# Token blocks of 512 in place of 384 in an attention and two-FFN kernel on one core

## The chip, the cores and the metric

The kernel runs on one core of a Trainium2 chip. The metric is device time in microseconds (us), the median of several executions. Engines are named as the profile does: PE is TensorE's matmuls, PEld its weight loads, DVE is VectorE, ACT is ScalarE, POOL is GpSimd, SP is SyncE, whose queue issues nearly all transfers. L93 is line 93 of the kernel file.

## What is computed

Attention over chunks of 32 queries with 8 memory keys, 16 keys of left and 8 of right context, for 4 batches, 8 heads, 768 tokens, 64 dimensions; then two feed-forward networks on the 3072 tokens, each 512 to 2048 to 512, in float32:

```
x   = attention(q, k, v, mem_k, mem_v)        # 3072 x 512
h   = x @ w_in1                               # up 1
x   = (s * max(h, 0)**2 + b) @ w_out1         # down 1
h   = x @ w_in2                               # up 2
out = (h - tanh(h)) @ w_out2                  # down 2
```

## The kernel before

Every product of the FFNs is made of three matmuls of float32r halves (`three`, L93 to L95): high weight by high token, low weight by high token, high weight by low token. Each loads its own 128 x 128 weights and streams NB = 384 tokens into one PSUM bank. The down products go through a seven-product scheme of the Winograd kind (P1 to P7): `combine` (L323, on POOL) makes the sums of up's outputs, which go through DRAM (o1, o2) to the down stages.

The stages follow each other, and a scheduler places every engine's instructions by readiness, so that work of one stage appears between that of another:

- Attention runs in 24 units of 128 tokens. `scores` (L181) makes 32 small matmuls into banks 0 and 1; VectorE adds the mask (L190), takes the maximum (L195), scales it (L196); ScalarE makes eight exponentials (L199), which read the scores with scale 0.125 and leave sums; VectorE adds 1e-9 to those sums (L204) and inverts them (L205); the product (L207) is on VectorE for the units of the first block and on POOL for the others. `transposes` (L215, L216) and `values` (L228) follow; ScalarE and VectorE split the result into halves xh and xl (L242, L243).
- Up 1 takes blocks of NB tokens, 16 tiles of 12 matmuls each. A tile is one bank of three (5 to 7). ScalarE's ReLU reads the bank and writes r (L317); VectorE squares r and scales it by s (L319). Attention units of the next block run between the tiles. The first block needs its units, three of them, before it can start, and eight weight conversions (`make_pair`, `to_f32`: L102 on ScalarE; L103, L104, L107 on VectorE; L276 on ScalarE; L277 on POOL).
- Eight quadrants of the down weights (L268 loads, the same conversion into zq) use the two raw buffers after the eight up weights.
- Down 1 and down 2 (`Down`) run through 7 products, 4 groups of 768 tokens, 2 halves of the depth, in 112 entries of 12 matmuls. Each entry's tokens are loaded, split by ScalarE (L411, L416) and VectorE (L412, L417) two entries ahead, into a ring of three. Four pairs of banks take the groups in turn. Products are combined by VectorE from the banks (L481 to L490, L591 to L600).
- Up 2 (L622 to L657) runs 8 weights by 4 groups, each two tiles of 24 matmuls, tanh on ScalarE (L637) and a subtraction on VectorE that reads the bank (L638).

All buffers are named places in one arena, E (2048 words), F (1536), Z (1024), G (768) and H (384).

Of the kernel before, what the change touches and what calls it, by code (L numbers as in the profile page):

```python
# [8 lines left out]
F32 = mybir.dt.float32  # L9
# [16 lines left out]
NB = 384  # L26
# [15 lines left out]
def tile_chunk_attention_two_ffn(  # L42
# [30 lines left out]
    SIZE = {"E": 2048, "F": 1536, "Z": 1024, "G": 768, "H": 384}  # L73

    def new(place, n, dt, name):
        assert n <= SIZE[place[0]], (place, n)
        return arena.tile([P, n], dt, tag=place, name=name)
# [19 lines left out]
    def to_f32(z, raw):  # L97
# [16 lines left out]
    A_QK, A_V = ("F8", "F9", "F10"), ("Z8", "Z9", "Z10")  # L114
    A_X = (("F0", "F1"), ("F2", "F3"))
    A_OT = (("F4", "F5"), ("F6", "F7"))
    A_PT, A_Z = ("Z11", "Z12"), ("Z13", "Z14")
    A_SM, A_R = ("G0", "G1"), ("H0", "H1", "H2")
    Z1 = {("A11", 0): "Z0", ("A11", 1): "Z1", ("A21", 0): "Z2", ("A21", 1): "Z3",
          ("A12", 0): "Z4", ("A12", 1): "Z5", ("A22", 0): "Z6", ("A22", 1): "Z7"}  # L120
    B_S = (("Z8", "Z9"), ("Z10", "Z11"))
    B_WHL = (("E8", "E9"), ("E0", "E1"))
    B_STREAM = ("F0", "F1", "E2", "E3")
    B_RING = (("F8", None), ("F9", None), ("F10", None))
    B_ACC = {"X": ("F2", "F3"), "U": ("F4", "F5"), "V": ("F6", "F7")}
# [12 lines left out]
    D_S = (("Z4", "Z5"), ("Z2", "Z6"))
    D_ACC = {"X": ("F6", "F2"), "U": ("F4", "F0"), "V": ("F1", "F8")}
    D_OUT = ("F9", "F10")  # L140
# [32 lines left out]
    def scores(u):  # L173
# [133 lines left out]
    def up1_tile(j, f, dst):  # L307
# [4 lines left out]
        ps = bank(5 + hcount[0] % 3)[:, 0:NB]  # L312
# [5 lines left out]
        r2 = r.rearrange("p (n t) -> p n t", n=2)  # L318
        nc.vector.scalar_tensor_tensor(out=dst, in0=r2, scalar=s_c[:, 0:1], in1=r2, op0=ALU.mult, op1=ALU.mult)  # L319
# [9 lines left out]
    class Down:  # L329
# [70 lines left out]
        def split(self, i):  # L400
            p, g, h, e = self.entries[i]
            src = self.view(self.part[i // 2], e)
            a, b_ = self.ring[i % len(self.ring)]
            if b_ is None:
                both = new(a, 4 * NB, F32R, "ring")
                xh, xl = both[:, 0:2 * NB], both[:, 2 * NB:4 * NB]
            else:
                xh, xl = new(a, 2 * NB, F32R, "ringh"), new(b_, 2 * NB, F32R, "ringl")
            xh, xl = (t.rearrange("p (x t) -> p x t", x=2) for t in (xh, xl))
# [41 lines left out]
    class Sums:  # L451
# [5 lines left out]
        def at(self, k, g):  # L457
            if (k, g // 2) not in self.t:
# [99 lines left out]
    def w2_load(n):  # L558
        w2[n] = load_raw(wi2, n, C_RAW)
# [168 lines left out]
```

## Time and profile before

| | us |
|---|---|
| three runs | 1148.92, 1149.27, 1150.51 |
| median | 1149.27 |
| span of the profiled execution, first to last instruction | 1147.0 |
| PE busy | 1101.0 |
| VectorE busy | 714.9 |
| ScalarE busy | 508.5 |
| POOL busy | 480.6 |

The profile is of one execution, for which only the span is given: the times of the runs also hold what surrounds the instructions. Busy time of PE counts overlapping matmuls once, so a PE that is busy throughout can still run at different speeds; the distance between starts tells that. A line of waits says which engine's instruction waited for which, the total, how often, and the longest.

### The profile page before, as it was taken

Reading aid. Unit: us, or ns where it says so; the run is one execution under the profiler, and the core shown is the slowest. Engines: PE = TensorE matmul, PEld = TensorE weight load, DVE = VectorE, ACT = ScalarE, POOL = GpSimd, SP = SyncE. Lnnn points to the kernel's source line nnn. Section 1 sums busy time; section 2 is a strip of 40 time slices with the busy share of each in tenths; the row PEclk is TensorE's granted clock in tenths of the full one; section 3 lists DMA queues with packets and bytes.
Section 4 is the critical chain, followed back from the end, with each engine's and each line's share of the span. In section 5 each row is a group of like instructions: output and inputs, shape, how many; then the busy total and the mean of one; then the engine's idle time right before and its main releaser. Section 6 shows DMA issues by size and latency. Waiting matters only on the chain.

```text
span 1147.0 us, 18807 instructions
## 1 busy us (share of the span) xinstructions
PE 1101.0 (96%) x7488; PEld 1075.3 (94%) x7488; DVE 714.9 (62%) x755; ACT 508.5 (44%) x973; POOL 480.6 (42%) x361
## 2 busy tenths in 40 slices
PE   3697899999999999999999999999999999999998
PEld 3596899999999999999999999999999999999998
DVE  5899855555555757668787654355522676677654
ACT  4664544444443345445565333222322454444442
POOL 2365754544548833111010256546756941111100
PEclk9998999999999999999999999999999999999999
DMA  8568665655623775555556366757644976667772
GB/s 329 181 222 305 240 218 198 217 190 200 219 111 146 257 259 172 190 189 193 193 187 218 122 225 242 256 201 249 239 189 164 321 235 192 187 214 224 246 232 83
DMA packets 91895, 242.39 MB, mean 211 GB/s; under 512 B 6560, under 2 KB 63904, under 8 KB 87712
## 3 DMA queue, kind: packets, MB, share of 16 engines
q1 hardware_dynamic: 91472, 240.02, 60.6%
q8 instruction: 58, 0.95, 0.3%
q10 hardware_dynamic: 336, 1.18, 0.3%
q14 instruction: 29, 0.24, 0.1%
HBM read 146.80 MB, written 94.37 MB: 210 GB/s over the span
## 4 chain that ended last, share of the span: by engine, by line
PE 85%; DVE 9%; DMA 2%; ACT 2%; issue 1%; SPq 0%; DVEq 0%; ACTq 0%
PE pb L93 27%; PE pb L95 27%; PE pb L94 27%; PE pb L228 2%; PE pb L215 2%; PE pb L181 1%; DMA raw<-in_wo_dram 1%; DVE oa L319 1%; DMA raw<-in_wi_dram 1%; DVE ring L412 1%; DVE z L107 1%; DVE z L104 1%; ACT sm L199 1%; DVE ringl L417 1%; DVE zq L104 1%
## 5 line engine op out<-in xcount | busy, mean ns | idle before, releaser
L93 PE MATMUL pb<-xh,w 128*128 128x384 f32 x512 | 179.1, 350 | 11.9 <-ACT r L317 7.6
L323 POOL TENSOR_TENSOR ob<-oa 128x384 f32<-128x384 f32 x128 | 148.8, 1163 | 94.0 <-DVE oa L319 68.2
L417 DVE TENSOR_TENSOR ringl<-part,ringh 128x768 fp32r<-128x768 f32 x112 | 137.1, 1237 | 68.2 <-ACT ringh L416 67.9
L94 PE MATMUL pb<-xh,w 128*128 128x384 f32 x512 | 173.8, 339 | 0.0
L95 PE MATMUL pb<-xl,w 128*128 128x384 f32 x512 | 173.1, 339 | 0.0
L94 PE MATMUL pb<-x2h,w 128*128 128x384 f32 x512 | 171.0, 334 | 0.0
L93 PE MATMUL pb<-x2h,w 128*128 128x384 f32 x512 | 170.8, 334 | 0.0
L319 DVE SCALAR_TENSOR_TENSOR oa<-r,s_c 128x384 f32<-128x384 f32 x128 | 118.5, 939 | 70.8 <-ACT r L317 59.5
L416 ACT ACTIVATE ringh<-part 128x768 fp32r<-128x768 f32 x112 | 94.9, 848 | 125.5 <-PE pb L94 120.7
L94 PE MATMUL pb<-ringh,whl 128*128 128x384 f32 x448 | 149.7, 334 | 0.0
L93 PE MATMUL pb<-ringh,whl 128*128 128x384 f32 x448 | 149.7, 334 | 0.0
L94 PE MATMUL pb<-ring,whl 128*128 128x384 f32 x448 | 149.7, 334 | 0.0
L93 PE MATMUL pb<-ring,whl 128*128 128x384 f32 x448 | 149.7, 334 | 0.0
L95 PE MATMUL pb<-ring,whl 128*128 128x384 f32 x448 | 132.9, 336 | 1.5 <-DVE ring L412 1.5
L95 PE MATMUL pb<-ringl,whl 128*128 128x384 f32 x448 | 132.7, 335 | 1.0 <-DVE ringl L417 0.9
L638 DVE TENSOR_TENSOR oa<-pb,r 128x768 f32<-128x768 f32 x64 | 60.4, 954 | 100.3 <-ACT r L637 85.5
L317 ACT ACTIVATE r<-pb 128x384 f32<-128x384 f32 x128 | 61.5, 488 | 133.3 <-PE pb L95 127.1
L323 POOL TENSOR_TENSOR ob<-oa,ob 128x384 f32<-128x384 f32 x64 | 72.6, 1135 | 114.1 <-DVE oa L638 73.3
L93 PEld LDWEIGHTS pb<-xh,w 128*128 128x128 f32 x512 | 97.9, 191 | 16.4 <-ACT r L317 8.4
L637 ACT ACTIVATE r<-pb 128x768 f32<-128x768 f32 x64 | 51.7, 812 | 129.0 <-PE pb L95 127.4
L395 POOL TENSOR_TENSOR whl<-s,whl 128x1024 fp32r<-128x1024 f32 x16 | 43.8, 2735 | 147.1 <-ACT whl L394 147.1
L412 DVE SCALAR_TENSOR_TENSOR ring<-part,b_c,ring 128x768 fp32r<-128x768 f32 x64 | 75.5, 1188 | 37.2 <-ACT ring L411 37.0
(93 smaller groups left out, 2239.9 us busy)
## 6 DMA issues: line engine op xcount, KB each, us to landing
o<-ob SPq DMA_DIRECT2D x64, 768.0 KB, 4.1
part<-o SPq DMA_DIRECT2D x112, 384.0 KB, 3.9
part<-o SPq DMA_DIRECT2D x56, 768.0 KB, 4.5
o<-oa SPq DMA_DIRECT2D x64, 576.0 KB, 3.4
raw<-in_wi_dram SPq DMA_DIRECT2D x16, 1024.0 KB, 6.4
raw<-in_wo_dram SPq DMA_DIRECT2D x16, 1024.0 KB, 6.5
qk<-in_qk_dram SPq DMA_DIRECT2D x24, 640.0 KB, 4.5
v<-in_vw_dram SPq DMA_DIRECT2D x21, 384.0 KB, 3.6
```

The lines of the kernel that those rows point to most:

```text
L93: nc.tensor.matmul(acc, lhsT=whi, rhs=xhi, start=first, stop=False)
L94: nc.tensor.matmul(acc, lhsT=wlo, rhs=xhi, start=False, stop=False)
L95: nc.tensor.matmul(acc, lhsT=whi, rhs=xlo, start=False, stop=last)
L317: nc.scalar.activation(out=r, in_=ps, func=AF.Relu)
L319: nc.vector.scalar_tensor_tensor(out=dst, in0=r2, scalar=s_c[:, 0:1], in1=r2, op0=ALU.mult, op1=ALU.mult)
L323: sub = lambda o, x, y: eng.tensor_tensor(out=o, in0=x, in1=y, op=ALU.subtract)
L395: eng.tensor_tensor(out=w[:, 1024:2048], in0=src, in1=w[:, 0:1024].bitcast(F32), op=ALU.subtract)
L412: nc.vector.scalar_tensor_tensor(out=xl, in0=src, scalar=self.bias, in1=xh.bitcast(F32), op0=ALU.add, op1=ALU.subtract)
L416: nc.scalar.activation(out=xh, in_=src, func=AF.Copy)
L417: nc.vector.tensor_tensor(out=xl, in0=src, in1=xh.bitcast(F32), op=ALU.subtract)
L637: nc.scalar.activation(out=r, in_=ps[:, :, 0:NB], func=AF.Tanh)
L638: nc.vector.tensor_tensor(out=oa[:, 2 * i:2 * i + 2], in0=ps[:, :, 0:NB], in1=r, op=ALU.subtract)
```

## The change

A block is 512 tokens, so every FFN matmul streams 512 columns into a whole bank. There are 6 blocks of up 1 in place of 8, 3 groups in place of 4 in both down stages and in up 2, 84 entries per down stage in place of 112, each still of 12 matmuls. The FFN matmuls are 4320 in place of 5760. The first block needs four attention units. Places are laid out anew: E and Z remain in the arena, the others lie in a side pool that holds Q, S, R (attention and ReLU buffers) until up 1 is through and Y (sums) after it. The pairs of float32r halves lie in one buffer or in two, as the place has room (`pair`).

The square in up 1 takes one factor from the bank and one from r, in place of both from r, so the bank is read twice. The mask's adding multiplies the scores by 0.125 as well, the maximum's own scaling is gone, and the exponentials take scale 1. Six of the eight down 1 quadrants are loaded in blocks 1 to 3 of the code and two in the last block; those of down 2 have raw buffers of their own.

```diff
-NB = 384
+NB = 512
...
-    SIZE = {"E": 2048, "F": 1536, "Z": 1024, "G": 768, "H": 384}
+    SIZE = {"E": 2048, "Z": 1024, "Y": 1024, "Q": 1280, "S": 768, "R": 512}
...
+    def swap_side(letters):
+        if "pool" in side:
+            side["pool"].__exit__(None, None, None)
+        side["pool"] = tc.tile_pool(name="side_" + letters[0], bufs=1, reuse_waits="tile")
+        side["of"] = side["pool"].__enter__()
...
-            nc.vector.tensor_tensor(
+            nc.vector.scalar_tensor_tensor(
                 out=sm[:, 4 * g:4 * g + 4, :], in0=bank(g)[:, 0:4 * KE].rearrange("p (r k) -> p r k", r=4),
-                in1=m4, op=ALU.add,
+                scalar=scale, in1=m4, op0=ALU.mult, op1=ALU.add,
             )
...
-        nc.vector.tensor_single_scalar(nmx, nmx, scale, op=ALU.mult)
...
-                bias=nmx[:, h:h + 1], scale=scale, accum_out=sums[:, h:h + 1],
+                bias=nmx[:, h:h + 1], scale=1.0, accum_out=sums[:, h:h + 1],
...
-        ps = bank(5 + hcount[0] % 3)[:, 0:NB]
+        ps = bank(5 + hcount[0] % 3)
...
-        r2 = r.rearrange("p (n t) -> p n t", n=2)
-        nc.vector.scalar_tensor_tensor(out=dst, in0=r2, scalar=s_c[:, 0:1], in1=r2, op0=ALU.mult, op1=ALU.mult)
+        ps2, r2 = (t.rearrange("p (n t) -> p n t", n=2) for t in (ps, r))
+        nc.vector.scalar_tensor_tensor(out=dst, in0=ps2, scalar=s_c[:, 0:1], in1=r2, op0=ALU.mult, op1=ALU.mult)
...
-                if 3 <= j <= 6 and i4 == 1 and q in (0, 2):
-                    thunks.append(down1.load_quadrant(A_RAW[q // 2]))
-                if 3 <= j <= 6 and i4 == 3 and q in (0, 2):
-                    thunks.pop()()
+                if (j in (1, 2, 3) and q in (0, 2)) or (j == NBLK - 1 and q in (0, 1)):
+                    if i4 == 1:
+                        thunks.append(down1.load_quadrant(A_RAW[1 if j == NBLK - 1 else q // 2]))
+                    if i4 == 3:
+                        thunks.pop()()
```

In the order that the scheduler gives, two places matter here. The first is TensorE's order up to the first FFN matmul. Scores have 64x96 operands, transposes 96x128, values 64x64; the numbers after qk, sm and v tell the units apart. Before, it ends so:

```order
L181 MATMUL pb_69<-qk_325 64x96 x16
L215 MATMUL pb_69<-ident_82,sm_278 96x128 x8
L228 MATMUL pb_69<-pt_251,v_117 64x64 x16
L181 MATMUL pb_69<-qk_403 64x96 x16
L228 MATMUL pb_69<-pt_329,v_123 64x64 x16
L93 MATMUL pb_69<-xh_243,w_133 128x384
```

Now it ends so:

```order
L247 MATMUL pb_69<-pt_326,v_123 64x64 x16
L201 MATMUL pb_69<-qk_399 64x96 x16
L234 MATMUL pb_69<-ident_82,sm_353 96x128 x8
L201 MATMUL pb_69<-qk_476 64x96 x8
L247 MATMUL pb_69<-pt_403,v_246 64x64
L234 MATMUL pb_69<-ident_82,sm_430 96x128 x4
L201 MATMUL pb_69<-qk_476 64x96 x3
L247 MATMUL pb_69<-pt_403,v_246 64x64 x15
L234 MATMUL pb_69<-ident_82,sm_430 96x128 x4
L201 MATMUL pb_69<-qk_476 64x96 x5
L234 MATMUL pb_69<-ident_82,sm_541 96x128 x4
L201 MATMUL pb_69<-qk_594 64x96 x8
```

Behind the values of the third unit (v_123) there now stand, ahead of the first FFN matmul, the values of a fourth (v_246), and scores and transposes of later units; in all 7.5 scores, 5.5 transposes and 4 values against 6, 3 and 3 (x16 of scores or values is one unit, x8 of transposes too).

The second is ScalarE's order within block 0: conversions of down weights (zq) among the ReLUs (r), the exponentials (sm) and the copies of attention (pt, xh). Before:

```order
L317 ACTIVATE r_703<-pb_69 128x384
L317 ACTIVATE r_720<-pb_69 128x384
L216 ACTIVATE pt_735<-pb_69 96x512 x2
L102 ACTIVATE zq_2505<-raw_2449 128x1024
L317 ACTIVATE r_754<-pb_69 128x384
L317 ACTIVATE r_804<-pb_69 128x384
L317 ACTIVATE r_835<-pb_69 128x384
L102 ACTIVATE zq_2762<-raw_2695 128x1024
```

Now:

```order
L336 ACTIVATE r_598<-pb_69 128x512
L336 ACTIVATE r_632<-pb_69 128x512
L116 ACTIVATE zq_2061<-raw_1984 128x1024
L336 ACTIVATE r_681<-pb_69 128x512
L261 ACTIVATE xh_590<-pb_69 128x4x128
L116 ACTIVATE zq_2306<-raw_2239 128x1024
L336 ACTIVATE r_718<-pb_69 128x512
L336 ACTIVATE r_733<-pb_69 128x512
```

Two or so ReLUs still stand between two conversions, but each is of a 512-column tile, and six conversions are here, where there were eight.

## Rows read from the trace of the kernel before

**Rows 1.** The page, part 1: TensorE's busy time, share, instructions
```profile
PE 1101.0 (96%) x7488; PEld 1075.3 (94%) x7488; DVE 714.9 (62%) x755; ACT 508.5 (44%) x973; POOL 480.6 (42%) x361
```

**Rows 2.** Busy times by stretch: length, PE, PEld, DVE, ACT, POOL, clock, DMA
```profile
52.10:142.00 89.90, 79.53 (x652) 74.05 (x652) 84.23 (x88) 47.94 (x122) 55.97 (x33) 0.94 0.70 245
142.00:440.00 298.00, 297.87 (x2503) 284.99 (x2504) 168.76 (x231) 139.42 (x419) 163.09 (x132) 1.00 0.55 199
```

**Rows 3.** Timeline of PE in down 1: start, duration in us
```profile
599.96 0.33 PE L93 MATMUL pb<-ring,whl 128*128 128x384 f32 x1
...
605.85 0.33 PE L95 MATMUL pb<-ring,whl 128*128 128x384 f32 x1
```

**Rows 4.** Timeline of PE at half clock, in block 0
```profile
107.36 0.52 PE L94 MATMUL pb<-xh,w 128*128 128x384 f32 x1
...
109.92 0.52 PE L93 MATMUL pb<-xh,w 128*128 128x384 f32 x1
```

**Rows 5.** Timeline of PE and PEld after an attention piece in up 1
```profile
265.60 0.19 PEld L93 LDWEIGHTS pb<-xh,w 128*128 128x128 f32 x1
265.71 0.19 PEld L94 LDWEIGHTS pb<-xh,w 128*128 128x128 f32 x1
265.88 0.34 PE L94 MATMUL pb<-xh,w 128*128 128x384 f32 x1
```

**Rows 6.** Timeline of PE in the opening: values, first FFN matmul
```profile
24.50 1.97 PE L228 MATMUL pb<-pt,v 96*64 96x64 f32 x30 [0.31 <-ACT pt L216]
...
45.85 1.98 PE L228 MATMUL pb<-pt,v 96*64 96x64 f32 x32 [2.49 <-DVE xl L243]
52.11 0.69 PE L93 MATMUL pb<-xh,w 128*128 128x384 f32 x1 [4.29 <-ACT xh L242]
```

**Rows 7.** The maximum's scaling, L196: duration ns min/median/max
```profile
L196 DVE TENSOR_SCALAR nmx<-nmx x24: 157/171/2361, 10.9 to 353.3; 128x8 f32<-128x8 f32 x24
```

**Rows 8.** Timeline of PE around values, and around transposes and scores
```profile
252.74 0.34 PE L95 MATMUL pb<-xl,w 128*128 128x384 f32 x1
...
254.37 0.34 PE L94 MATMUL pb<-xh,w 128*128 128x384 f32 x1
...
259.57 0.34 PE L94 MATMUL pb<-xh,w 128*128 128x384 f32 x1
...
262.52 0.34 PE L94 MATMUL pb<-xh,w 128*128 128x384 f32 x1
```

**Rows 9.** Groups by line, PE, 52.1 to 142 us: count, busy us, mean ns
```profile
L93 PE MATMUL pb<-xh,w 128*128 128x384 f32 x108 | 40.0, 371 | 11.7 <-ACT r L317 7.4 <-ACT xh L242 4.3
...
L215 PE MATMUL pb<-ident,sm 128*96 128x128 f32 x40 | 6.6, 320 | 2.9 <-POOL sm L207 2.9
L228 PE MATMUL pb<-pt,v 96*64 96x64 f32 x160 | 6.3, 226 | 0.0
L181 PE MATMUL pb<-qk 64*64 64x96 f32 x128 | 3.9, 250 | 0.0
```

**Rows 10.** Waits, 52 to 142 us: total us, times, longest
```profile
ACT zq L102 <- DMA raw<-in_wo_dram: 17.7, 7, 6.1
...
PE pb L93 <- ACT r L317: 7.4, 3, 3.8
```

**Rows 11.** Timeline of SP: issues of raw down weights, first and eighth
```profile
68.72 0.33 SPq L268 DMA_DIRECT2D raw<-in_wo_dram  x1
...
121.05 0.33 SPq L268 DMA_DIRECT2D raw<-in_wo_dram  x1
```

**Rows 12.** Timeline at the end: the last VectorE instruction
```profile
1142.68 0.95 DVE L596 TENSOR_TENSOR o<-sumU,pb 128x768 f32<-128x768 f32 x1 [4.58 <-PE pb L95]
```

**Rows 13.** VectorE reading a bank, 512 columns, L243: duration ns min/median/max
```profile
L243 DVE TENSOR_TENSOR xl<-pb,xh x24: 632/680/692, 35.8 to 371.4; 128x512 fp32r<-128x512 f32 x24
```

**Rows 14.** The page, part 5: a down split's VectorE half
```profile
L417 DVE TENSOR_TENSOR ringl<-part,ringh 128x768 fp32r<-128x768 f32 x112 | 137.1, 1237 | 68.2 <-ACT ringh L416 67.9
```

**Rows 15.** Waits, 142 to 440 us
```profile
DVE sums L204 <- ACT sm L199: 37.2, 16, 3.4
```

More of the change, by code (lines that the diff above doesn't have):

```diff
@@ L69, in tile_chunk_attention_two_ffn @@
     pb = psum.tile([P, 8 * 512], F32, name="pb")
-    SIZE = {"E": 2048, "F": 1536, "Z": 1024, "G": 768, "H": 384}
+    SIZE = {"E": 2048, "Z": 1024, "Y": 1024, "Q": 1280, "S": 768, "R": 512}
+    side = {}
+    def swap_side(letters):
[3 more added lines that the diff above has]
+        side["of"] = side["pool"].__enter__()
+        side["letters"] = letters
+    swap_side("QSR")
+    ctx.callback(lambda: side["pool"].__exit__(None, None, None))
     def new(place, n, dt, name):
         assert n <= SIZE[place[0]], (place, n)
-        return arena.tile([P, n], dt, tag=place, name=name)
+        if place[0] in "QSRY":
+            assert place[0] in side["letters"], place
+        pool = arena if place[0] in "EZ" else side["of"]
+        return pool.tile([P, n], dt, tag=place, name=name)
     def bank(k):
@@ new lines, in tile_chunk_attention_two_ffn, with pair @@
+    D_WHL = (("E8", "E10"), ("E2", "E3"))
+    D_STREAM = ("E0", "E1", "E6", "E14", "E17")
+    D_RING = (("Z5", "Z11"), "E13", "E16")
+    D_S = (("Z9", "Z10"), ("Z2", "Z3"))
+    D_ACC = {"X": ("Z7", "Z8", "Z4"), "U": ("Z6", "Z0", "Z1"), "V": ("Y0", "Y1", "E7")}
+    D_OUT = ("E9", "E15")
+    def pair(place, n, names):
+        if isinstance(place, tuple):
+            return tuple(new(p_, n, F32R, nm) for p_, nm in zip(place, names))
+        both = new(place, 2 * n, F32R, "".join(names))
+        return both[:, 0:n], both[:, n:2 * n]
@@ L402, in split @@
             src = self.view(self.part[i // 2], e)
[L403 to L409, printed above, removed]
+            xh, xl = (
+                t.rearrange("p (x t) -> p x t", x=2)
+                for t in pair(self.ring[i % len(self.ring)], 2 * NB, ("ringh", "ringl"))
+            )
             if self.bias is not None and ORDER[p] in ("P1", "P2", "P3", "P6"):
@@ L457, in at @@
         def at(self, k, g):
-            if (k, g // 2) not in self.t:
-                self.t[k, g // 2] = new(self.places[k][g // 2], 4 * NB, self.dt, f"sum{k}")
-            o = 2 * NB * (g % 2)
-            return self.t[k, g // 2][:, o:o + 2 * NB].rearrange("p (m t) -> p m t", m=2)
+            place = self.places[k][g]
+            if (k, place) not in self.t:
+                n = 2 * NB * self.places[k].count(place)
+                self.t[k, place] = new(place, n, self.dt, f"sum{k}")
+            o = 2 * NB * (g - self.places[k].index(place))
+            return self.t[k, place][:, o:o + 2 * NB].rearrange("p (m t) -> p m t", m=2)
     def load1(dst, name, g, h):
@@ L466, in load1 @@
             nc.sync.dma_start(
[L467 removed]
+                out=dst[:, 2 * NB * jj:2 * NB * (jj + 1)].rearrange("p (q t) -> p q t", q=2),
                 in_=o1[2 * g + jj][:, 2 * h:2 * h + 2, SLOT[name], :],
             )
[L471 to L472 removed]
+    sums1 = Sums(B_ACC, F32)
+    x2 = {}
     def final1(name, g, ps):
@@ L477, in last_sum @@
         def last_sum(k, x, op):
-            o = new(B_TMP[n_tmp[0] % 2], 2 * NB, F32, "x2").rearrange("p (m t) -> p m t", m=2)
-            n_tmp[0] += 1
+            o = a(x)
+            if k == "Q":
+                o = new(B_TMP[g], 2 * NB, F32, "q").rearrange("p (m t) -> p m t", m=2)
             nc.vector.tensor_tensor(out=o, in0=a(x), in1=ps, op=op)
-            hi = new(B_HI[k][g], 2 * NB, F32R, "x2h").rearrange("p (m t) -> p m t", m=2)
+            hi, lo = (
+                t.rearrange("p (m t) -> p m t", m=2) for t in pair(X2[k][g], 2 * NB, ("x2h", "x2l"))
+            )
             nc.scalar.activation(out=hi, in_=o, func=AF.Copy)
-            lo = lows1.at(k, g)
             nc.vector.tensor_tensor(out=lo, in0=o, in1=hi.bitcast(F32), op=ALU.subtract)
@@ L645, in tile_chunk_attention_two_ffn @@
                 w2_make(n + 1)
-            if g == 2 and n < 4:
-                thunks.append(down2.load_quadrant(C_RAW))
-            if g == 3 and n < 4:
-                thunks.pop()()
-            if n in (4, 5, 6) and g in (2, 3):
-                if down2.quads:
-                    down2.load_quadrant(C_RAW)()
+            if g == 0 and 1 <= n <= 4:
+                thunks.extend(down2.load_quadrant(C_RAW[1 + i]) for i in range(2))
+            if g in (1, 2) and thunks:
+                thunks.pop(0)()
             if n == 7 and g in (1, 2):
```

55 lines of the change are left out of this document (23 added, 32 removed).

## The prediction

> **What bounds the kernel now.** I began with the busy time per engine: TensorE works for 1101.0 of 1147.0 us [rows 1]. That share hides two regimes, so I then read the busy times by stretch [rows 2]. From 142 us TensorE never pauses (297.87 of 298.00 us), and no other engine sets the time. Between 52.1 and 142 us VectorE is the one without a pause (84.23 of 89.90), TensorE stands for a tenth of the stretch, and its clock falls to 0.94 on average. Before 52.1 us no FFN matmul has run at all.
>
> In the saturated part the question is what one matmul costs, and its duration does not answer that, since matmuls overlap. The timeline does: 34 matmuls of 384 columns start between 599.96 and 605.85 us [rows 3], 173.2 ns apart. At 2.4 GHz 384 columns take 160 ns, so 13.2 ns of each step are not columns. Where the clock is at its lower level, 1.2 GHz, eight steps take 2.56 us [rows 4], 320 ns each, which is 384 columns and nothing else. So the 13.2 ns show at full clock only, and one size cannot say what they depend on. There are three readings: a fixed amount per matmul; an amount that grows with the columns; or a floor of about 173 ns that a longer matmul would clear. For the floor speaks that a weight load (0.19 us) lasts about as long as a step. Against it: after a pause, the load at 265.60 lets the next load begin at 265.71 and the second matmul at 265.88 [rows 5]. With a step of 173 between the two matmuls the first must have begun near 265.71, 0.11 us after its own load began, so weights are ready long before 160 ns are over. I take the fixed amount.
>
> **The matmuls.** Blocks of 512 leave the columns alone and cut the FFN matmuls from 5760 to 4320. Before: 5760 x 0.1732 = 997.6 us. After, with the same 13.2 ns on 213.3 ns of columns: 4320 x 0.2265 = 978.5 us. The gain is 1440 x 13.2 ns = **19.1 us**. The ends are the other two readings: 0.1732 x 512/384 = 0.2309, which gains nothing, and 213.3 ns without any extra, 921.5 us, which gains 76.
>
> The Trainium skill ("TensorE: Matmul & The Clock Gate", section "Wait — 56ns, not 53.3ns?") also has an extra that vanishes at the low clock, and the same one at 128 and 512 columns, but of 2.5 ns. By that rule 4320 steps would take 215.8 ns each, 932 us in all. The trace differs already at 384 columns: the rule would give 162.5 ns, the row 173.2.
>
> **The opening.** Block 0 of up 1 needs four attention units in place of three. Values matmuls of units 0 to 2 start 24.50 to 45.85 us, 10.7 us apart, and the first FFN matmul at 52.11 [rows 6]. A fourth unit at that pace would give 62.8. The scale in the mask's adding removes the tiny scaling of the maximum, which usually takes 0.17 us but up to 2.36 [rows 7] when VectorE is held up; I give it back 2 to 3 us in the opening and take **60 us**, so +7.9. Bounds: 56, if the new order packs better (the weight conversions fill VectorE's pauses), and 68, if the one to two more weight conversions that now stand ahead of the fourth unit on VectorE all count.
>
> Part of this is work that no longer has to be done later. In the order, 7.5 score groups, 5.5 transposes and 4 values stand ahead of the first FFN matmul, against 6, 3 and 3. Prices from the timeline: values push the matmuls apart by 1.63 less two steps = 1.28 us; transposes and scores together by 2.95 less six steps (1.04) = 1.91 us, about 0.9 and 1.0 [rows 8]. So 1.5 x 1.0 + 2.5 x 0.9 + 1.28 = **-5.0 us**.
>
> **Blocks 0 and 1.** Between 52.1 and 142 us 108 x 3 FFN matmuls ran, and 5 transposes, 5 values, 4 score groups [rows 9]: 324 x 0.1732 + 5 x 1.28 + 4 x 1.91 + 0.9 = 71.0 us. So 18.9 of 89.9 us were lost. The waits name the cause: ScalarE waits 17.7 us for raw down weights, and TensorE's first matmuls of a tile wait for the ReLU that frees their bank [rows 10]. ScalarE runs in order, so a ReLU behind a conversion that waits for its transfer waits too. Transfers of the eight quadrants are issued from 68.72 to 121.05 us, 7.5 us apart [rows 11]; there are two raw buffers, so each waits for a conversion. The order lets about two ReLUs through per conversion: two tiles, 24 x 0.1732 = 4.2 us and 1.2 us of attention (3 units x 3.19 over 16 tiles). 5.4 against 7.5 loses 2.1 a time, eight times 17 us, near the 18.9. After: two tiles take 24 x 0.2265 = 5.4 us and 1.6 us of attention (4 units over 16 tiles), 7.0 against 7.5; and only six quadrants come here, two now in the last block. 0.5 x 6 = 3 us, the 2 us that the estimate lacked above, and 3 us because the square now reads the bank, so the bank is free one VectorE instruction later. I take **8 us lost, so -10.9**. Bounds: 4, and 19 as now.
>
> **The rest.** The last VectorE add takes 0.95 us for 768 columns [rows 12]; 1024 add about 0.3, the last store as much: **+0.5 us**. The square at 512 columns from the bank has a near row, a subtraction of 512 columns from the bank at 0.680 us [rows 13]; it is cover work, TensorE needs 2.7 us a tile. In the down stages a split's VectorE half takes 1.24 us for 768 columns [rows 14], about 1.6 for 1024, under twelve matmuls of 2.7 us (2.1 now): the same share, nothing on the path. Without that cover it would cost the difference at each of 168 splits. In the new order up 2's first half that uses the last down 1 group's bank is put behind its sister half, so that hand-over costs nothing. Token loads and stores keep their bytes.
>
> **The sum:** -19.1 + 7.9 - 5.0 - 10.9 + 0.5 = -26.6 us, against the profiled span of 1147.0: 1120.4. The median of the runs, 1149.27, lies 2.3 us above that span, for what surrounds it; the forecast is 1149.27 - 26.6 = **1123 us**. Within this case the opening (-4 to +8) and block 0 (-4 to +11) give 1114 to 1143.
>
> **Rivals.**
>
> *Floor or a smaller extra:* a step of 215.8 ns. 932.3 in place of 978.5: 46 us less, **1077 us**. For it speaks the length of the weight load, and that the extra vanishes at half clock, as a floor would; against it, that weights were ready in 0.11 us. It needs no other change than TensorE's step. The page named above would have this result. Chance 0.13.
>
> *Extra by columns:* a step of 230.9 ns; the -19.1 goes and the rest stays, **1142 us**, with the opening's bounds 1133 to 1161. For it: nothing in the trace excludes that columns come a little slower than the clock at full speed. Against: at 1.2 GHz they come at exactly the clock. Chance 0.15.
>
> *The bank is held (slower):* in up 1 a bank used to be free after the ReLU; now the square on VectorE frees it. VectorE runs in order, and its softmax sum waits for the eight exponentials, 37.2 us in 16 waits, the longest 3.4 [rows 15]. A square behind that wait holds its bank. With three banks it must end within two tiles, 5.4 us, of its matmuls; the point at which it decides is where ReLU, exponentials, sum and square come together behind one tile. A unit that loses 1.8 us makes the kernel slower (29 us over the 16 units after block 0); 3.4 each is 54 us, **1177 us**. Against it: TensorE's two tiles have become longer by a third while the exponentials have not. [...] Chance 0.07.
>
> *The edit gives nothing:* all terms at their bad ends, or a wait that no row shows: within 0.2% or slower. Chance 0.03.
>
> **How the numbers follow.** The forecast case has 0.62. A time within 0.2% (about what a measurement of this kernel can tell from no change) is 1147.0 to 1151.6. Faster: 0.62 + 0.13 + 0.10 of the second rival = 0.85. The same: 0.03 of that rival and 0.02 of the last, 0.05. Slower: 0.07 + 0.02 + 0.01 = 0.10. The range leaves out the floor rival (0.13) and the held bank (0.07): from 1108, a little under the best of the forecast case, to 1150, which takes in most of the columns rival.
>
> **What would show it.** Right: steps of 226 to 227 ns in the saturated stretches, and 4320 FFN matmuls; the first FFN matmul at 56 to 68 us; lost time between it and 142 us under 10 us; no new wait of TensorE in up 1 for the square. Wrong: steps of 216 or 231 ns decide between the first two rivals at one look; a wait of TensorE's L107 for VectorE at L338, once per attention unit, would be the held bank; steps at 1.2 GHz in the middle of up 1 would go with it.

## The result, and the profile after

The changed kernel takes **1132.47 us** (median of four runs, 1132.05 to 1132.94), the kernel before 1149.54 beside it (1148.92 to 1150.51). The ratio is 0.9849, with a 95% interval of 0.9835 to 0.9863: faster by 17 us, where 26.6 were forecast. 1132.47 lies inside the range. The span of the profiled execution is 1131.1 us, against 1147.0.

The page of the changed kernel, part 1 (busy time, share of the span, instructions):

```profile
PE 1089.1 (96%) x6048; PEld 887.4 (78%) x6048; DVE 643.0 (57%) x610; ACT 489.4 (43%) x863; POOL 466.4 (41%) x296
```

TensorE's share is what it was [rows 1], but the share of weight loads fell from 94 to 78%: 1440 loads are gone. Busy times by stretch:

```profile
60.00:142.00 82.00, 73.41 (x519) 56.78 (x519) 60.97 (x65) 38.35 (x100) 41.98 (x24) 0.94 0.68 245
142.00:440.00 298.00, 298.00 (x2116) 236.96 (x2115) 132.09 (x186) 134.89 (x378) 154.66 (x106) 1.00 0.57 204
640.00:917.00 277.00, 277.00 (x1224) 229.38 (x1223) 130.91 (x96) 83.62 (x82) 184.42 (x112) 1.00 0.61 229
```

In the two later stretches TensorE again has no pause. In the first, which begins 3 us ahead of the first FFN matmul, it still stands for a tenth of the time, at a mean clock of 0.94. VectorE, which paused for 5.7 of 89.9 us there before [rows 2], now pauses for 21 of 82.

The step, from the timeline of PE in up 2. 34 steps of one matmul lie between these two starts, 226.7 ns each; [rows 3] gave 173.2 at 384 columns, and the mean over all steps that the table below uses is 173.3:

```profile
699.96 0.39 PE L107 MATMUL pb<-x2h,w 128*128 128x512 f32 x1
...
707.67 0.39 PE L108 MATMUL pb<-x2hx2l,w 128*128 128x512 f32 x1
```

The opening, from the timeline of PE: the third and fourth unit's values, and the first FFN matmul at 63.09, where it was 52.11 [rows 6]. The first matmuls are 0.43 us apart, which is 512 columns at 1.2 GHz.

```profile
41.94 1.98 PE L247 MATMUL pb<-pt,v 96*64 96x64 f32 x32 [3.94 <-DVE xl L262]
...
55.95 1.97 PE L247 MATMUL pb<-pt,v 96*64 96x64 f32 x30
...
63.09 0.80 PE L107 MATMUL pb<-xh,w 128*128 128x512 f32 x1
...
64.54 0.63 PE L108 MATMUL pb<-xh,w 128*128 128x512 f32 x1
64.97 0.63 PE L107 MATMUL pb<-xh,w 128*128 128x512 f32 x1
```

Between there and 142 us, the groups of PE by line (the counterpart of [rows 9]), and the waits (of [rows 10]):

```profile
L107 PE MATMUL pb<-xh,w 128*128 128x512 f32 x77 | 32.6, 423 | 3.6 <-DVE oa L338 3.5
...
L247 PE MATMUL pb<-pt,v 96*64 96x64 f32 x160 | 6.1, 225 | 0.0
L234 PE MATMUL pb<-ident,sm 128*96 128x128 f32 x28 | 4.7, 322 | 4.5 <-POOL sm L226 4.5
L201 PE MATMUL pb<-qk 64*64 64x96 f32 x82 | 4.5, 288 | 0.0
```

```profile
ACT zq L116 <- DMA raw<-in_wo_dram: 15.6, 5, 5.5
...
PE pb L234 <- POOL sm L226: 4.5, 1, 4.5
```

230 FFN matmuls at 226.7 ns, 3.5 transposes, 5 values and 2.6 score groups at the prediction's prices make 64.3 of the 78.9 us. So **14.6 us are lost here**; it was 18.9, and the forecast said 8. A third of it is one pause of 4.5 us at 109 us. Timelines of DVE, POOL and PE around it:

```profile
103.10 0.54 DVE L210 SCALAR_TENSOR_TENSOR sm<-pb,mask_mid 128x384 f32<-128x384 f32 x1
...
104.91 0.94 DVE L215 TENSOR_REDUCE nmx<-sm 128x8 f32<-128x768 f32 x1
105.77 0.68 DVE L117 TENSOR_SCALAR zq<-zq 128x1024 int32<-128x1024 int32 x1
106.49 3.30 DVE L118 SCALAR_TENSOR_TENSOR zq<-raw,zq 128x1024 int32<-128x1024 int32 x1
109.82 2.17 DVE L121 SCALAR_TENSOR_TENSOR zq<-raw,zq 128x1024 int32<-128x1024 int32 x1
111.92 0.16 DVE L223 TENSOR_SCALAR sums<-sums 128x8 f32<-128x8 f32 x1
```

```profile
105.83 2.88 POOL L414 TENSOR_TENSOR whl<-zq,whl 128x1024 fp32r<-128x1024 f32 x1
108.67 2.24 POOL L342 TENSOR_TENSOR ob<-ob,oa 128x512 f32<-128x512 f32 x1
112.48 1.47 POOL L226 TENSOR_TENSOR sm<-sm,rs 128x768 f32<-128x768 f32 x1 [1.57 <-DVE rs L224]
```

```profile
108.94 0.55 PE L201 MATMUL pb<-qk 64*64 64x96 f32 x12
114.01 1.94 PE L234 MATMUL pb<-ident,sm 128*96 128x128 f32 x8 [4.52 <-POOL sm L226]
```

Read it backwards. The transposes wait for GpSimd's normalised probabilities, these for the sum (L223) on VectorE. The exponentials were done at 108.8, but two instructions of one conversion of raw down weights (L118, L121) stand ahead of the sum, and they last 3.30 and 2.17 us, each beside a GpSimd instruction. L118's shortest is 1.21 us (below, in e5). GpSimd's own order counts too: it is busy with the down weights' low half (L414) and a combine (L342) until 110.91, so a sum in time would have saved 1.6 of the 4.5 us, the idle time in the row of L226.

The pause also costs clock. Behind it TensorE runs for 3.4 us at 1.2 GHz, a granted share of 0.50 (the third column from the end):

```profile
113.90:117.30 3.40, 3.29 (x29) 2.65 (x30) 1.11 (x3) 1.19 (x2) 3.01 (x4) 0.50 0.98 325
```

From 108.62 to 117.03 us no FFN matmul starts; less one step and the prices of the scores and transposes in between, this one gap loses 6.3 of the 14.6 us. In the kernel before, 23 steps between FFN matmuls of block 0 have the 320 ns of [rows 4] in place of 173.3, which is 3.4 us of the 18.9; now there are 5, of 427 ns, for 1.0 us.

### The profile page after: what moved, and what is told of

Same layout as the page of the kernel before. It is cut to its first block, busy times and chain, and to the rows that moved or that the text cites. A ratio compares the mean times of both kernels' runs of the same rounds, so it can differ in the third digit from the quotient of the medians.

```text
span 1131.1 us, 15257 instructions
## 1 busy us (share of the span) xinstructions
PE 1089.1 (96%) x6048; PEld 887.4 (78%) x6048; DVE 643.0 (57%) x610; ACT 489.4 (43%) x863; POOL 466.4 (41%) x296
## 4 chain that ended last, share of the span: by engine, by line
PE 90%; DVE 6%; DMA 2%; ACT 1%; issue 1%; POOL 0%; POOLq 0%; SPq 0%; ACTq 0%; DVEq 0%
PE pb L107 29%; PE pb L109 28%; PE pb L108 28%; PE pb L247 2%; PE pb L201 2%; PE pb L234 1%; DVE z L118 1%; DMA raw<-in_wo_dram 1%; DVE zq L121 1%; ACT sm L218 1%; DVE sm L210 1%; DVE nmx L215 1%; DMA qk<-in_qk_dram 1%; DVE z L121 1%; DVE zq L118 0%
## 5 line engine op out<-in xcount | busy, mean ns | idle before, releaser
L107 PE MATMUL pb<-ringhringl,whl 128*128 128x512 f32 x560 | 217.9, 389 | 0.0
L108 PE MATMUL pb<-ringhringl,whl 128*128 128x512 f32 x560 | 217.9, 389 | 0.0
L109 PE MATMUL pb<-ringhringl,whl 128*128 128x512 f32 x560 | 195.8, 389 | 0.0
L342 POOL TENSOR_TENSOR ob<-oa 128x512 f32<-128x512 f32 x96 | 141.7, 1479 | 88.0 <-DVE oa L660 46.5
L433 DVE TENSOR_TENSOR ringhringl<-part,ringhringl 128x1024 fp32r<-128x1024 f32 x92 | 127.9, 1391 | 84.6 <-ACT ringhringl L432 84.6
L107 PE MATMUL pb<-xh,w 128*128 128x512 f32 x384 | 156.7, 408 | 3.6 <-DVE oa L338 3.5
L432 ACT ACTIVATE ringhringl<-part 128x1024 fp32r<-128x1024 f32 x92 | 97.7, 1062 | 136.4 <-PE pb L109 123.9
L109 PE MATMUL pb<-xl,w 128*128 128x512 f32 x384 | 150.7, 393 | 0.0
L108 PE MATMUL pb<-xh,w 128*128 128x512 f32 x384 | 150.7, 392 | 0.0
L338 DVE SCALAR_TENSOR_TENSOR oa<-pb,s_c,r 128x512 f32<-128x512 f32 x96 | 71.6, 748 | 109.7 <-ACT r L336 107.2
L108 PEld LDWEIGHTS pb<-ringhringl,whl 128*128 128x128 f32 x560 | 105.1, 188 | 21.9
L107 PEld LDWEIGHTS pb<-ringhringl,whl 128*128 128x128 f32 x560 | 105.1, 188 | 21.9
L109 PEld LDWEIGHTS pb<-ringhringl,whl 128*128 128x128 f32 x560 | 105.1, 188 | 21.7
L414 POOL TENSOR_TENSOR whl<-s,whl 128x1024 fp32r<-128x1024 f32 x16 | 41.5, 2592 | 133.7 <-ACT whl L413 133.7
L342 POOL TENSOR_TENSOR ob<-oa,ob 128x512 f32<-128x512 f32 x48 | 68.1, 1418 | 66.5 <-DVE oa L660 40.4
L428 DVE SCALAR_TENSOR_TENSOR ringhringl<-part,b_c,ringhringl 128x1024 fp32r<-128x1024 f32 x48 | 71.7, 1501 | 37.2 <-ACT ringhringl L427 37.1
L107 PE MATMUL pb<-x2hx2l,w 128*128 128x512 f32 x224 | 87.2, 389 | 0.0
```

The costliest lines, as they stand in the source:

```text
L107: nc.tensor.matmul(acc, lhsT=whi, rhs=xhi, start=first, stop=False)
L108: nc.tensor.matmul(acc, lhsT=wlo, rhs=xhi, start=False, stop=False)
L109: nc.tensor.matmul(acc, lhsT=whi, rhs=xlo, start=False, stop=last)
L338: nc.vector.scalar_tensor_tensor(out=dst, in0=ps2, scalar=s_c[:, 0:1], in1=r2, op0=ALU.mult, op1=ALU.mult)
L342: sub = lambda o, x, y: eng.tensor_tensor(out=o, in0=x, in1=y, op=ALU.subtract)
L428: nc.vector.scalar_tensor_tensor(out=xl, in0=src, scalar=self.bias, in1=xh.bitcast(F32), op0=ALU.add, op1=ALU.subtract)
```

## Where the 15.8 us of the span came from

Each row below splits a profiled span, from the start times of all matmuls in the trace: until the first FFN matmul; the FFN matmuls times their step (998.4 us at 384, 979.2 at 512 columns); the gaps between FFN matmuls in which attention's matmuls stand, with whatever was waited for there; what other gaps exceed the step by; and the rest at the end. "Time" is the median of the runs, "before" the median of the kernel before beside it.

| kernel | time | before | first FFN | FFN | attention, with waits | other gaps | end |
|---|---|---|---|---|---|---|---|
| before | 1149.5 | | 52.1 | 998.4 | 74.5 | 17.5 | 4.5 |
| changed | 1132.5 | 1149.5 | 63.1 | 979.2 | 71.8 | 11.5 | 5.5 |
| e1 square from r | 1138.9 | 1150.4 | 62.7 | 979.2 | 75.1 | 13.2 | 5.5 |
| e2 scale apart | 1131.1 | 1150.4 | 61.8 | 979.2 | 66.9 | 15.9 | 5.5 |
| e3 small edits at 384 | 1151.0 | 1150.4 | 46.7 | 998.4 | 83.3 | 16.6 | 4.5 |
| e4 down weights later | 1122.6 | 1150.4 | 62.6 | 979.2 | 63.6 | 9.7 | 5.2 |
| e5 lo on VectorE | 1121.8 | 1150.5 | 55.0 | 979.2 | 67.1 | 12.5 | 5.2 |
| e8 e4 and e1 | 1122.8 | 1150.5 | 62.9 | 979.2 | 63.7 | 10.7 | 5.3 |
| e9 e4 and e5 | 1115.1 | 1150.1 | 55.5 | 979.2 | 63.5 | 9.8 | 5.3 |
| e10 e9, four pairs | 1117.4 | 1150.1 | 53.0 | 979.2 | 68.0 | 11.1 | 5.1 |
| e11 e4 and e5 at 384 | 1139.8 | 1150.2 | 48.8 | 998.4 | 63.6 | 20.3 | 4.4 |
| e12 e9, scale apart | 1119.5 | 1150.2 | 58.7 | 979.2 | 64.6 | 10.2 | 5.2 |

So: opening +11.0, FFN -19.2, attention and other gaps together -8.7, end +1.1.

## The experiments

**e1, the square from r alone.**

```diff
-        ps2, r2 = (t.rearrange("p (n t) -> p n t", n=2) for t in (ps, r))
-        nc.vector.scalar_tensor_tensor(out=dst, in0=ps2, ...)
+        r2 = r.rearrange("p (n t) -> p n t", n=2)
+        nc.vector.scalar_tensor_tensor(out=dst, in0=r2, ...)
```

> The changed kernel, its square taken from r alone again, so that the ReLU frees the bank and VectorE reads two operands of SBUF. Theory (the step of the matmuls carries the gain, the square's source is nearly nothing): 1130 to 1135 us; TensorE's four waits for the square between 63 and 142 us (3.5 us together) turn into waits for the ReLU of about the same length, the square takes longer than the 748 ns it has now wherever GpSimd works beside it (it was 939 ns at 384 columns before), and the time lost in the steady part of up 1 (150 to 350 us, 6.6 us over the pitch) stays between 5 and 8. Rival A (a bank held by the square costs): 1126 to 1129, the steady part back to under 4 us lost. Rival B (the relief of VectorE is a large part of the gain): 1138 or more, and TensorE waits for VectorE in up 1.

1138.94 us (1137.49 to 1140.31): 6.5 above the changed kernel, rival B's number but not its place. The square's durations (min/median/max ns) in the steady part, of the changed kernel and of e1:

```profile
L338 DVE SCALAR_TENSOR_TENSOR oa<-pb,s_c,r x57: 737/751/753, 143.9 to 349.3; 128x512 f32<-128x512 f32 x57
```

```profile
L338 DVE SCALAR_TENSOR_TENSOR oa<-r,s_c x55: 734/753/2052, 145.5 to 346.0; 128x512 f32<-128x512 f32 x55
```

From the bank the square has a fixed length. From SBUF 33 of the 55 are as short; the 22 longer ones all have a GpSimd instruction beside them, and so have 11 of the short ones. TensorE has no wait for either in that part. Of the 4.5 us by which its span is longer, 2.1 are the pause at 109 us, now 6.7 us long, and 1.5 a wait for VectorE's xl (L262) at 367 us; the rest lies in small pieces, and the median of its runs lies 3.3 us above its profiled span where that of the changed kernel lies 1.3. e8 tests whether the square matters where that pause is gone.

**e2, the softmax scale apart again.**

```diff
-            nc.vector.scalar_tensor_tensor(... scalar=scale, in1=m4, op0=ALU.mult, op1=ALU.add)
+            nc.vector.tensor_tensor(... in1=m4, op=ALU.add)
+        nc.vector.tensor_single_scalar(nmx, nmx, scale, op=ALU.mult)
```

> The changed kernel with the softmax scale apart again: a plain addition of the mask, and the maximum scaled by an instruction of its own. Theory (my prediction's step): the tiny scaling costs 2 to 3 us in the opening where it is held up, so the first FFN matmul comes at 65 to 66.5 us in place of 63.1 and the time is 1134 to 1136 us; nothing changes after 142 us. Rival (the instruction fills a pause of VectorE): first FFN matmul within 0.5 us of 63.1, 1132 to 1133 us.

1131.09 us (1129.86 to 1131.18), first FFN matmul at 61.8. Neither expectation held: the instruction that was to cost 2 to 3 us in the opening came with an opening 1.3 us earlier. The order of the other instructions shifts too, and in place of the 4.5 us pause for the transposes TensorE has eight waits for the square up to 123 us, 7.9 us in all, the longest 2.0. In this kernel the price of the edit is smaller than what a shift of order makes.

**e3, the two small edits at 384 columns**: the diffs of e1 and e2 turned round, in the kernel before.

```diff
+                scalar=scale, in1=m4, op0=ALU.mult, op1=ALU.add,
-        nc.vector.tensor_single_scalar(nmx, nmx, scale, op=ALU.mult)
...
+        nc.vector.scalar_tensor_tensor(out=dst, in0=ps2, ...)
```

> The kernel before, blocks of 384 and its buffers as they were, with the two small edits alone: scale in the mask's addition, square from the bank. Theory (the step of 226.7 in place of 230.9 ns per 512 columns carries the gain): 1143 to 1148 us: the opening up to 2.5 us earlier, the lost time of block 0 up to 3 us less, and the FFN step still 173.2 ns. Rival A (the small edits are most of the 17 us): 1131 to 1137 us. Rival B (with only two tiles of 4.2 us in reserve the held bank delays TensorE in steady up 1): 1152 us or more, with waits of TensorE for the square once per attention unit.

1150.97 us (1148.19 to 1153.87), ratio 1.001 [0.9999, 1.002]: no change, between the expectations. But the parts moved: the first FFN matmul came 5.4 us earlier, at 46.7, and attention with its waits took 8.8 us more. In e3's waits from 46 to 142 us stands

```profile
PE pb L93 <- DVE oa L318: 8.5, 6, 3.2
```

which is the held bank of my slower rival, in block 0 alone; after 142 us TensorE waits for nothing. So the small edits give nothing at 384: what the opening gains, block 0 gives back. Which of the two edits moves which part was not separated.

**e4, down 1 weights held behind their tile.** A load may overwrite its raw buffer only when a small GpSimd instruction has written there, and that one reads the output of the tile at which the program asks for the load.

```diff
     def load_raw(src, n, place, behind=None):
         raw = new(place, 2048, I32, "raw")
+        if behind is not None:
+            nc.gpsimd.tensor_tensor(out=raw.bitcast(F32)[:, 0:256], in0=behind, in1=behind, op=ALU.subtract)
...
-    thunks.append(down1.load_quadrant(A_RAW[...]))
+    thunks.append(down1.load_quadrant(A_RAW[...], oa[:, 0, 0, :]))
```

> The changed kernel with each raw down 1 weight load of up 1 held behind the tile at which the program asks for it (a GpSimd write of 256 elements into the raw buffer that reads that tile's output, computed as x minus x), so that no conversion of down weights stands in block 0 any more; they start in block 1, where TensorE has no pauses. Theory (conversions that wait for their transfer on the in-order ScalarE, and their three VectorE instructions ahead of a softmax sum, are the main loss between the first FFN matmul and 142 us, now 14.6 us): 5 to 8 us of these go, 1124 to 1128 us; the pause of 4.76 us at 109 us is gone, ScalarE's wait for raw in 63 to 142 us falls from 15.6 to under 4. Rival A (the loss comes from the softmax chain and GpSimd's work, the conversions only fill gaps): 1131 to 1134 us, the pauses stay. Rival B (the loss only moves with the conversions into blocks 1 to 3): 1130 to 1135, with new pauses of TensorE between 130 and 320 us.

**1122.59 us** (1122.08 to 1124.34), 9.9 below the changed kernel and a little better than expected. Its pauses of TensorE between 63 and 142 us are one wait of 0.3 us:

```profile
PE pb L107 <- DVE oa L340: 0.3, 1, 0.3
```

The lost time there, worked out as above (266 FFN matmuls, 4.5 transposes, 5.1 values, 3.6 score groups in 79.4 us), is 5.0 us in place of 14.6. The first conversions now stand at 133, 163, 192 and 224 us, 29 to 32 us apart, and nowhere from the first FFN matmul to 400 us are two starts of TensorE's matmuls more than 0.7 us apart. The loss did not move, it went: both rivals fall. That the early conversions of down weights cost 9.6 us of block 0 is shown. The gap at 109 us, which lost 6.3, loses 0.3 here, and the waits for the square, 3.5 us in all, are down to 0.3. The edit moves the loads, ScalarE's and VectorE's conversions and GpSimd's low halves together, so what each of them cost is not shown.

**e5, the low halves of up 1's weights on VectorE.**

```diff
-            make_pair(raws.pop(n), A_Z[n % 2], A_W[n], 1, n)
+            make_pair(raws.pop(n), A_Z[n % 2], A_W[n], 1, n, lo_pool=False)
```

> The changed kernel with the low halves of the up 1 weights computed on VectorE in place of GpSimd. In the changed kernel VectorE has no pause from 23.9 to 57.4 us, and five of its instructions there last 1.3 to 2.2 us longer than their kind does alone, each beside a GpSimd subtraction. Theory (this contention sets the opening): 9 us of stretching go and five subtractions of about 1.2 us come, so the first FFN matmul comes at 59 to 61 us in place of 63.1 and the time is 1127 to 1131 us. Rival A (VectorE's load itself sets the opening, whoever does the low halves): 63 to 67 us, 1132 to 1137. Rival B (the exponentials on ScalarE set it): within 0.5 us of 63.1, 1131 to 1134.

**1121.75 us** (1121.2 to 1125.36), 10.7 below the changed kernel; first FFN matmul at 55.0, 8 us earlier, four more than expected. One conversion's durations from 20 to 63 us, in the changed kernel, and there the GpSimd subtraction beside it:

```profile
L118 DVE SCALAR_TENSOR_TENSOR z<-raw,z x6: 1210/2231/3396, 23.9 to 61.5; 128x1024 int32<-128x1024 int32 x6
```

```profile
L296 POOL TENSOR_TENSOR w<-z,w x6: 2348/2648/3339, 23.1 to 60.5; 128x1024 fp32r<-128x1024 f32 x6
```

and in e5 the same two:

```profile
L118 DVE SCALAR_TENSOR_TENSOR z<-raw,z x6: 1216/1218/1631, 23.6 to 60.3; 128x1024 int32<-128x1024 int32 x6
```

```profile
L296 DVE TENSOR_TENSOR w<-z,w x6: 1212/1222/1226, 24.7 to 58.3; 128x1024 fp32r<-128x1024 f32 x6
```

GpSimd's help costs VectorE more than the work that it takes off: from 23.9 us to 57.4 six instructions of the changed kernel last 9.6 us longer than their kind's shortest, and in e5 VectorE does the five subtractions itself in 6.1 us, with 0.4 us of stretching left. That is 3 of the 8 us. The rest comes with the order of the other instructions, which shifts as well, and is not separated. The Trainium skill ("SBUF — State Buffer", section "Who interferes with whom") says that a VectorE instruction with two SBUF inputs contends with a GpSimd instruction that reads SBUF; the durations of L118 agree, and so do the square's in e1. A single SBUF input is no safeguard in every case, though. The square with its other operand in a bank keeps its length (737 to 753 ns, above), but L117, whose one input is z, lasts 2.84 us beside the subtraction that starts at 29.72, against 0.63 at its shortest:

```profile
29.78 2.84 DVE L117 TENSOR_SCALAR z<-z 128x1024 int32<-128x1024 int32 x1
```

**e6, short matmuls.** Each FFN matmul of up 1 is cut into two of 256 columns, each of up 2 into four of 128.

```diff
-        for c in range(KD):
-            three(ps, wh[:, i, c, :], wl[:, i, c, :], xh[:, c, :], xl[:, c, :], c == 0, c == KD - 1)
+        for cut in (slice(0, 256), slice(256, 512)):
+            for c in range(KD):
+                three(ps[:, cut], wh[:, i, c, :], wl[:, i, c, :], xh[:, c, cut], xl[:, c, cut], ...)
```

> The changed kernel with each FFN matmul of up 1 cut into two of 256 columns and each of up 2 into four of 128, each with its own weight load; the down stages keep 512. It measures the step against the columns. Theory (13.2 to 13.3 ns per matmul whatever its columns): 119.9 ns in steady up 1 and 66.5 ns in up 2, where a weight load that lasts 0.19 us does not set the pace; time +20 us for up 1 and +48 for up 2, about 1200 us. Rival A (the extra goes with the columns, 0.4427 ns each): 113.3 and 56.7 ns, the time stays near 1132. Rival B (a floor of 160 to 175 ns per matmul that the weight load sets, which 384 and 512 columns both showed with something else on top): 160 ns and more in both, up 1 about 90 us and up 2 several hundred us longer.

Timeline of PE, in up 1 (17 steps) and in up 2 (45 steps):

```profile
248.05 0.28 PE L107 MATMUL pb<-xh,w 128*128 128x256 f32 x1
...
250.09 0.28 PE L109 MATMUL pb<-xl,w 128*128 128x256 f32 x1
```

```profile
799.90 0.27 PE L107 MATMUL pb<-x2h,w 128*128 128x128 f32 x1
...
804.92 0.27 PE L107 MATMUL pb<-x2hx2l,w 128*128 128x128 f32 x1
```

At 256 columns the step is 120.0 ns, the theory's 119.9: the extra is 13.3 ns at 256, 384 and 512 columns. At 128 the step is 111.6 ns, not 66.5, so there is a floor, but below 120 ns: far from the 160 and more that rival B wanted. The kernel took 1381 us (one run) against my 1200, which should have been 1193 (at the theory's own steps up 1 grows by 15 us and up 2 by 45, not 20 and 48). Up 2's 4 x 1152 = 4608 short matmuls at 45 ns above the forecast are 208 us of the difference, and something that I had not thought of gives 24 back. A half of 256 columns needs only two attention units, so the first FFN matmul comes at

```profile
39.11 0.58 PE L107 MATMUL pb<-xh,w 128*128 128x256 f32 x1 [1.24 <-ACT xh L261]
```

in place of 63.09.

**e7, two weight pairs ahead of block 0.**

```diff
-        if len(agenda) % 3 == 0:
+        if len(agenda) % 3 == 0 and w_made[0] < 2:
```

> The changed kernel with only two of the eight up 1 weight pairs converted ahead of block 0; the other six are made in block 0, in front of the tiles that need them. Theory (the opening is VectorE's: five to six pairs at 3.1 us and the stretching beside GpSimd stand in it, and the same work then stands in block 0, where two tiles last 5.4 us and a pair with its softmax share and squares takes VectorE 6 to 8): first FFN matmul at 49 to 55 us, lost time between it and 142 us larger by about as much, 1129 to 1137 us. Rival A (block 0 hides the conversions): 1121 to 1126. Rival B (the opening is bound by the chain of the four units themselves): first FFN matmul at 60 or later.

1132.95 us (1131.65 to 1133.51), first FFN matmul at 63.0. This run tells nothing of the question: the scheduler orders by its own estimate of time, and made the same order on every engine as for the changed kernel. It is a repeat of that kernel, and shows how well the time repeats (0.5 us). To move a conversion, its data must come later, as in e4 and e10.

**e8, e4 with the square from r**: both diffs together.

```diff
+    thunks.append(down1.load_quadrant(A_RAW[...], oa[:, 0, 0, :]))
...
+        nc.vector.scalar_tensor_tensor(out=dst, in0=r2, ...)
```

> Both earlier edits: down 1 weights held behind their tile (1122.6 us alone) and the square taken from r alone (1138.9 us alone, against 1132.5 of the changed kernel). Theory (the square's source costs only through the pause at 109 us, which the longer square of two SBUF operands lengthened from 4.76 to 6.91 us and which is gone without the early conversions): 1120 to 1125 us. Rival (the bank read relieves VectorE by itself, in every block): 1127 to 1131 us, with waits of TensorE for VectorE in the steady part.

1122.80 us (1122.29 to 1123.59), against 1122.59: the same. The square's source, worth 6.5 us in e1, is worth nothing once the conversions have left block 0.

**e9, e4 and e5 together.**

```diff
+            make_pair(raws.pop(n), A_Z[n % 2], A_W[n], 1, n, lo_pool=False)
...
+    thunks.append(down1.load_quadrant(A_RAW[...], oa[:, 0, 0, :]))
```

> Both edits that helped: down 1 weights held behind their tile (-10 us alone) and the low halves of up 1's weights on VectorE (-11 us alone). Theory (two causes in two places, the opening and block 0): they add up, first FFN matmul near 55 us, no pause of TensorE over 1 us after it, 1111 to 1115 us. Rival (both remove the same loss, the delays of block 0): 1118 to 1122 us.

**1115.12 us** (1114.62 to 1115.3), ratio to the kernel before 0.9694 [0.9681, 0.9707], 17.4 us below the changed kernel. The fastest of the kernels here; the two gains add up but for 3 us. No wait of TensorE is left after the first FFN matmul, at 55.5 us:

```profile
55.00:142.00 87.00, 87.00 (x660) 68.51 (x660) 46.34 (x70) 43.23 (x128) 40.10 (x28) 0.98 0.55 197
```

**e10, e9 with only four pairs ahead of block 0**: the raw loads of the last four pairs wait for block 0's last tokens, and the program asks for them only behind the opening.

```diff
+            late = x_t[0][0][:, 3, 256:512].bitcast(F32) if n >= 4 else None
-            raws[n] = load_raw(wi1, n, A_RAW[n % 2])
+            raws[n] = load_raw(wi1, n, A_RAW[n % 2], late)
...
-        if len(agenda) % 3 == 0:
-            w1_load()
+        if len(agenda) % 3 == 0 and w_made[0] < 4:
+            if w_loaded[0] < 4:
+                w1_load()
```

> As the run with both edits, and the raw loads of up 1's last four weight pairs are held behind block 0's last tokens (a GpSimd write that reads them), so that four pairs, not six, can be converted ahead of the first FFN matmul. It asks what still bounds the opening. Theory (VectorE's load, of which a pair with its low half is 4.3 us): the first FFN matmul comes 4 to 8 us earlier than in the run with both, at 47 to 51 us, and block 0 hides the late pairs in part: 1106 to 1113 us. Rival (the chain scores, softmax, transposes, values of four units sets it): first FFN matmul within 1.5 us of that run, and the time the same or longer, 1111 to 1118 us.

1117.39 us (1116.76 to 1118.62). The first FFN matmul came only 2.5 us earlier, at 53.0, between the expectations. That speaks against VectorE's load as the main bound of the opening once the contention is gone, but does not show what is. And block 0 gave back 5.8 us, among it one wait of 3.7:

```profile
PEld pb L234 <- POOL sm L226: 3.7, 1, 3.7
```

**e11, e4 and e5 at 384 columns**: the same lines in the kernel before, where the loads are asked for in blocks 3 to 6.

```diff
+            nc.gpsimd.tensor_tensor(out=raw.bitcast(F32)[:, 0:192], in0=behind, in1=behind, op=ALU.subtract)
...
+            make_pair(raws.pop(n), A_Z[n % 2], A_W[n], 1, n, lo_pool=False)
```

> The kernel before, blocks of 384 and everything else as it was, with the two edits that helped the changed kernel: down 1 weights held behind their tile, low halves of up 1's weights on VectorE. With the losses of the opening and of block 0 gone on both sides, the two block sizes can be compared (the changed kernel with both: 1115.1 us). Theory (my terms: 19.2 us from the matmul step, the opening of a fourth unit about 8 dearer in 512, 5 of it work done ahead): 384 is slower by 15 to 18, 1130 to 1134 us. Rival (the two edits help only the changed kernel, whose block 0 they fit): 1140 to 1149 us.

1139.78 us (1137.4 to 1141.89), ratio 0.9916 [0.9899, 0.9932], between the expectations. Attention with its waits fell to 63.6 us, as at 512, which fits the same cause in block 0 for both sizes. But TensorE stands idle for 5.1 us between 325 and 400 us, at the end of up 1, where two of the held conversions wait for their transfers too and TensorE's waits name

```profile
PE pb L93 <- ACT r L319: 4.8, 3, 3.1
```

so the 25 us between e11 and e9 are no clean price of the block size. 19.2 of the 22.2 us between their spans are the FFN column.

**e12, e9 with the softmax scale apart**: the diff of e2 on e9.

```diff
+        nc.vector.tensor_single_scalar(nmx, nmx, scale, op=ALU.mult)
```

> The changed kernel with both edits and the softmax scale apart again (alone this was 1.4 us faster than the changed kernel, where 2 to 3 slower was expected). Theory (that 1.4 was the pause at 109 us, which the other order broke into smaller ones, not the price of the instruction): with the pause gone the extra instruction costs at most its time on VectorE, four units of 0.2 us ahead of the first FFN matmul: 1114.5 to 1116.5 us. Rival (scaling in the mask's addition is the slower form, as its instruction is longer): 1112 to 1114 us.

1119.52 us (1119.07 to 1121.48), 4.4 above e9, more than expected; 3.2 of it are the opening. The merged scale is worth having here, while in e2 it was not: its price hangs on what stands beside it.

## Why the prediction was right, and where it was off

- **The matmuls, -19.1: right, -19.2.** A fixed extra: 226.7 ns against 226.5. e6 settles it with a third size. The prediction's argument against the floor, weights ready in 0.11 us, took the first matmul of [rows 5] to start at 265.71, a step before the second, where the trace lists it at 265.60 with its load; e6 bears the 0.11 us out, as the distance of both loads and matmuls at 128 columns. The floor rival (215.8 ns) and the extra by columns (230.9) both fall. The Trainium skill's page on TensorE ("TensorE: Matmul & The Clock Gate", section "Wait — 56ns, not 53.3ns?") has the form right, an extra that does not depend on the columns; its 2.5 ns would give 215.8, and these matmuls took 226.7.
- **The opening, +7.9: measured +11.0.** The pace of units alone gave 62.8; the failed step is "I give it back 2 to 3 us" for the tiny scaling. e2 has its opening at 61.8 with the scaling in. In another order the merging does pay: in e12 the scaling costs 3.2 us of opening. That the pace came so near is in part luck, since the units themselves were slowed by something that the prediction did not name: the stretching of VectorE beside GpSimd's low halves. I had seen it only as the scaling's 2.36 us [rows 7]; taking it away makes the opening 8 us shorter, 3 of them accounted for (e5).
- **Attention ahead, -5.0, and blocks 0 and 1, -10.9: -8.7 together.** Of these, the lost time up to 142 us gives 14.6 - 18.9 = -4.3, and the rest, -4.4, answers to the -5.0. The failed step is the size of **"I take 8 us lost"**. Its cause was right: e4 takes the early conversions away, and the loss falls to 5.0. But I let longer tiles cover the transfer (7.0 us of work against 7.5), as if a conversion could only delay a ReLU. ScalarE still waits 15.6 us for raw weights, near the 17.7 of before [rows 10], and I left out the second path: the conversion's VectorE instructions stand ahead of a softmax sum, stretched by GpSimd to 5.5 us, and the transposes wait for that. A third term stood at nothing without a reason, the clock: 3.4 of the 18.9 us lost before went to steps at 1.2 GHz, so that the 17 us worked out for the conversions came so near to 18.9 was in part chance. And the 3 us for the bank read are not borne out: TensorE waits 3.5 us for the square, but e1, whose square leaves the bank alone, loses as much outside the gap at 109 us (8.6 of 17.0 us, the changed kernel 8.6 of 14.9, both counted gap by gap).
- **The end, +0.5: +1.1.** The last add takes 1.22 us, against 0.95 [rows 12].
- **The bank held: right that it would not bind** in up 1's steady part at 512. TensorE's waits for the square are 3.5 us, all before 142 us.
- **The signs.** Steps, matmul count and first FFN matmul came as the prediction said a right one would show them. Two did not: lost time under 10 us (14.6), and no new wait for the square, which block 0 has. The time lies in the range because the matmuls' term was exact and the range was wide, not because opening and block 0 were well priced.
- The sum was short by 10.8 us of span (3.1 opening, 7.2 block 0 and attention, 0.6 end, less 0.1); the median is 9.5 off, since the runs of the changed kernel lie 1.3 us above its span, where I had taken 2.3.

Still open: what bounds the opening below 53 us with blocks of 512 (the chain of four units was not tried alone; cutting block 0's matmuls alone into halves, which e6 suggests, was not tried either), and what in the order decides whether the merged scale helps.

## What to carry to other kernels

Take the step between matmuls at full clock from the trace, and split it into columns and a rest: the rest is what larger blocks save, and a second regime (half clock) helps to tell them apart. For a stretch in which several engines lose time in turn, do not cost an early, not yet needed load by the engine that waits for its transfer alone; list every instruction that it puts ahead of others on each in-order engine, and what GpSimd does beside it. And giving an engine's work to GpSimd can slow the giver by more than it saves: 1.2 us of VectorE against up to 2.2 us of stretching in one instruction.

## What the runs showed of the hardware

The extra of a float32r matmul with its own weight load is 13.3 ns at 256, 384 and 512 columns (120.0, 173.3, 226.7 ns), and nothing at 1.2 GHz ([rows 4]). At 128 columns the step is 111.6 ns, 58 above the columns' 53.3. The weight loads there start 0.11 us apart too, each listed with 0.19 us; that they set the floor was not tested.
